# Token projections moved out of a memory chain, and transposes of a bulk stage spread and merged

## The chip, the cores and the metric

The kernel runs on one core of a Trainium2 chip, as one program, and computes a forward pass and all gradients. A core has TensorE (matmuls and transposes; in the profile PE, with its weight loads as PEld), VectorE (DVE), ScalarE (ACT), GpSimd (POOL) and SyncE (SP). SP only issues DMAs here; POOL computes and issues DMAs too. Transfers issued by SP appear under SPq. The metric is the device time of the program in microseconds (us), lower is better. The times stand for single executions; the profile shows one more execution.

## The reference, cut to what matters

A gate mixes two attentions over the same input, S = 2048 tokens of D = 576. Attention A is multi-query attention: 32 heads of 18, one shared key and value. Attention B is recurrent: 64 segments of 32 tokens, each preceded by 8 memory tokens that the segment before has produced; 32 heads of 128. The output is the forward result and the gradients of all inputs and weights (twelve arrays).

```python
def _A_ref(x, wq, wk, wv, wo):               # S = 2048, D = 576, H = 32, Dh = 18
    q = (x @ wq) in 32 heads;  k = x @ wk;  v = x @ wv
    p = _softmax(einsum('bhqd,bkd->bhqk', q, k) * Dh ** (-0.5))
    return heads_joined(einsum('bhqk,bkd->bhqd', p, v)) @ wo
def _B_ref(x, mem0, Wq, Wk, Wv, Wo, seg_len):  # M = 8, seg = 32, H = 32, Dh = 128
    mem = mem0
    for s in range(n_seg):                     # 64
        h = jnp.concatenate([mem, xs], axis=1)
        q, k, v = (einsum('btd,dhe->bhte', h, W) for W in (Wq, Wk, Wv))
        p = _softmax(where(mask, einsum('bhqe,bhke->bhqk', q, k) * scale, -1e9))
        o = einsum('bhte,hed->btd', einsum('bhqk,bhke->bhqe', p, v), Wo)
        mem = o[:, :M, :].copy();  outs.append(o[:, M:, :])
g = _sigmoid((x * gate_w).sum(-1, keepdims=True))
out = g * _A_ref(...) + (1 - g) * _B_ref(...)   # and its vjp with grad_out
```

(The listing is condensed; reshapes are left out.)

## The kernel before

`build_full` runs stages one after the other, each with its own SBUF and PSUM pools. In most of them a scheduler orders the instructions on each engine; the two woven stages and the bulk stage have their order written out by hand (`manual_schedule`), so their instructions go to each engine in the order of the Python code.

1. Preparation (`prep`), the setup of attention A (`a_weights`, `a_setup`, and `a_qd_all`, which projects queries and their gradients for 16 head pairs and 4 blocks of 512 tokens and stores them by SP), then `make_WoT`.
2. `b_proj_x(("dO",), ...)`: the output gradient of B times the transpose of Wo, for 16 tiles of 128 tokens. Each tile loads x transposed (`p_x`), runs 8 column groups of 512 with 5 k-tiles each (576 = 4 x 128 + 64; the last k-tile is filled up with zeros to 128 rows, both in the weights and in the tokens), evacuates `p_pb` in turns by DVE and ACT into `p_tok`, and stores it by SP. In each tile three pieces of W are transposed by DMA (`stash_WT`, 48 in all: SP transposes into `p_wt`, POOL stores `st_WT`) for use in the backward chain.
3. `load_W`, then `b_proj_x(("k", "v", "q"), ..., XT0)` with XT0 = 5: the same projection for the first 5 tiles, three weights each.
4. The forward chain of B, woven one to one with the first attention pass of A (`weave`: one piece of `b_chain_fwd`, one of `a_pass1`, 1024 pieces of the latter). The chain projects a segment's 8 memory tokens with Wk, Wq and Wv (`proj_part`): the 4096 columns are split into four quarters which sit in the four 32-column groups of the array, so the stationary operand `hm` has 32 columns, 8 of memory and 24 free. The free 24 columns carry ("ride") 24 of the tokens from tile 5 on, in every segment: 64 segments x 24 columns cover the remaining 11 tiles. `load_ride` brings them in; `rows_out` dumps the whole result to `row_dram` by POOL, and `rows_copy` copies from there, by SP, memory rows to `mtok` and token rows to `xtok`.
5. `a_out` (output projection of A: one token tile is loaded as `o_ot`, transposed on PE by `tok_T`, evacuated, multiplied in `row_mm` in columns 0 to 512 and 512 to 576) and `b_mem_fwd`.
6. `b_bulk`: the token rows of B, forward and backward, in 128 ticks of one token tile and a group of 4 heads. Nine stages work on successive groups, and each tick runs them in a fixed order: `st_QT` (transposes of q, k and dO on PE into PSUM tiles `x_tr`, which have two buffers), `st_S` (scores, exponentials on ACT, row sums and reciprocals on DVE), `st_T` (transposes of P), `st_O`, `st_OT` (transposes of o), `st_D`, `st_B`, `st_DT` (transposes of dS), `st_Q`, `st_K`. `transp`, used by `st_T` and `st_DT`, transposes four token blocks of 128 x 128 and four blocks of 128 x 32 memory scores, the latter one by one into the four row groups of a fifth block.
7. The backward chain of B woven with the second pass of A (it also uses `proj_part`), then `b_post`, `b_dw` and `a_final`, which again transposes token tiles with `tok_T` and multiplies them in `row_mm`.

`mm` (line 66 of the profile) and `tr` (line 71) are helpers that issue all matmuls and transposes, and `evac` (lines 61 and 63) copies PSUM to SBUF by DVE or ACT. The names in the profile tell which stage an instruction belongs to: p_ the dense projections, c_ the forward chain, a_ the attention A, x_ the bulk stage, o_ and z_ the stage after the chain, r_ the backward chain, f_ the final stage.

Of the kernel before, what the change touches and what calls it, by code (L numbers as in the profile page):

```python
# [11 lines left out]
P = 128  # L12

D = 576
# [16 lines left out]
class Kern:  # L31
# [50 lines left out]
    XT0 = 5  # L82

    def setup_B_dram(self, dram):
# [13 lines left out]
        self.row_dram = {w: t(w + "row_dram", [NSEG, P, 1024]) for w in ("k", "q", "v")}  # L98
# [13 lines left out]
    def zero_fill(self, sp):  # L112
        nc = self.nc
        z = sp.tile([P, 16, P], BF16, name="zfill")
        nc.gpsimd.memset(z[:], 0.0)
        for tt in range(self.NTT):
            nc.gpsimd.dma_start(self.pq_dram[tt].rearrange("s q c w k -> (s q c) w k"), z[:])

# [40 lines left out]
    def load_W(self, pool):  # L159
        nc = self.nc  # L160
        self.W = {}
        for w, src in (("k", self.B_Wk), ("q", self.B_Wq), ("v", self.B_Wv)):
            t = pool.tile([P, NKT, J], BF16, name="W" + w)
            nc.vector.memset(t[64:128, 4, :], 0.0)
            for kt in range(NKT):
                rows = KT_ROWS[kt]
                self.dq_eng().dma_start(t[0:rows, kt, :], src[kt * P:kt * P + rows, :])
            self.W[w] = t
# [13 lines left out]
    def b_proj_x(self, ws, srcT, sp, psum, ntt):  # L182
        nc = self.nc
        for tt in range(ntt):
            if len(ws) == 1:
                for c in range(3 * tt, 3 * tt + 3):
                    self.stash_WT(c, sp)
            xt = sp.tile([P, NKT, P], BF16, name="p_x", bufs=3)
            nc.sync.dma_start(xt[:], srcT[:, :, tt * P:(tt + 1) * P].rearrange("k p t -> p k t"))
            for w in ws:  # L190
                Wt = self.WoT if w == "dO" else self.W[w]
                tok = sp.tile([P, J], BF16, name="p_tok", bufs=2)
                for jc in range(8):
                    pb = psum.tile([P, 512], F32, name="p_pb", bufs=8)
                    for kt in range(NKT):
                        self.mm(pb[:], lhsT=xt[:, kt, :], rhs=Wt[:, kt, jc * 512:(jc + 1) * 512],
# [19 lines left out]
    def proj_part(self, pj, st, Wt, j, kts):  # L216
        for kt in kts:
            for c in range(4):
                self.mm(pj[32 * c:32 * c + 32, :], lhsT=st[:, kt, :],
                        rhs=Wt[:, kt, c * 1024 + j * 512:c * 1024 + (j + 1) * 512],  # L220
# [13 lines left out]
    def b_chain_fwd(self, keep, sp, psum):  # L234
# [8 lines left out]

        def ride(s):
            t0 = self.XT0 * P + 24 * s
            return t0, max(0, min(24, self.T - t0))

        def load_ride(s):
            t0, n = ride(s)
            if n:  # L250
                nc.sync.dma_start(hm[s % 2][:, :, 8:8 + n], self.xT_dram[:, :, t0:t0 + n].rearrange("k p t -> p k t"))

        load_ride(0)
# [14 lines left out]
        for s in range(NSEG):  # L268
# [8 lines left out]
            def rows_out(w):  # L277
                nc.gpsimd.dma_start(self.row_dram[w][s], t2[w][:].rearrange("p u e -> p (u e)"))

            def rows_copy(w):  # L280
                src = self.row_dram[w][s].rearrange("(c r) e -> c r e", r=32)
                t0, n = ride(s)
                nc.sync.dma_start(self.mtok[w][s * 8:(s + 1) * 8, :].rearrange("r (c e) -> c r e", c=4), src[:, 0:8, :])
                if n:
                    nc.sync.dma_start(self.xtok[w][t0:t0 + n, :].rearrange("r (c e) -> c r e", c=4), src[:, 8:8 + n, :])
# [9 lines left out]
            for j in range(2):  # L295
                proj("k", j)
                if j == 0 and s + 1 < NSEG:
                    load_ride(s + 1)
# [13 lines left out]
            rows_copy("k")  # L312
# [29 lines left out]
            rows_copy("q")  # L342
# [12 lines left out]
            if s + 1 < NSEG:  # L355
# [13 lines left out]
                rows_copy("v")  # L369
# [17 lines left out]
            else:  # L387
                yield
                rows_copy("v")
# [49 lines left out]
    def make_WoT(self, pool, psum):  # L439
        self.WoT = pool.tile([P, NKT, J], BF16, name="WoT")  # L440
        self.nc.vector.memset(self.WoT[64:128, 4, :], 0.0)
# [10 lines left out]
    def load_WoT(self, pool):  # L452
        self.WoT = pool.tile([P, NKT, J], BF16, name="WoT")
        self.nc.vector.memset(self.WoT[64:128, 4, :], 0.0)
# [9 lines left out]
    def b_bulk(self, wp, sp, psum):  # L464
# [76 lines left out]
        def transp(x, m, nm):  # L541
# [3 lines left out]
            for i in range(4):  # L545
                self.tr(pt[32 * i:32 * i + 32, 4, :], m[:, i, :], P, tp=(0, 32 * i))
# [14 lines left out]
        def st_QT(t):  # L561
            tt, g, r, d = view(t)
            for w, nb in (("q", 3), ("k", 3), ("dO", 6)):
                pt = psum.tile([P, 5, P], BF16, name="x_tr", bufs=2)
                for i in range(4):
                    self.tr(pt[:, i, :], d[w][:, 4 * (g % 4) + i, :], P)
                o = sp.tile([P, 4, P], BF16, name=f"x_{w}T", bufs=nb)
                self.evac(o[:], pt[:, 0:4, :], use="s" if w == "dO" else "v")
                sc[w + "T", t] = o
# [112 lines left out]
        order = list(enumerate(stages)) + [(6, st_K)]  # L682
        with self.tc.manual_schedule():
# [8 lines left out]
            for t in range(NG + len(stages) - 1):  # L692
                for n, st in order:
                    if 0 <= t - n < NG:
                        st(t - n)
                    if (n != 6 or st is st_K) and n in after and t - n >= 0 and (t - n) % 4 == 3:
# [40 lines left out]
    def b_chain_bwd(self, keep, sp, psum):  # L737
# [11 lines left out]
        def load(s):  # L749
# [15 lines left out]
            for w in ("k", "q"):  # L765
                nc.sync.dma_start(mrow[w][:].rearrange("p u e -> p (u e)"), self.row_dram[w][s])
# [345 lines left out]
    def setup_A_dram(self, dram):  # L1112
# [5 lines left out]
        self.dqtok_dram = dram.tile([T, D], BF16, name="dqtok_dram")  # L1118
        self.otok_dram = dram.tile([T, D], BF16, name="otok_dram")
# [20 lines left out]
    def prep(self, keep, xk, sp, psum):  # L1140
# [11 lines left out]
        nc.gpsimd.memset(self.daT[64:128, 4, :], 0.0)  # L1152
# [79 lines left out]
    def a_setup(self, keep, sp, psum):  # L1232
# [3 lines left out]
        for lo in range(0, T, 512):  # L1236
            pk = psum.tile([P, 512], F32, name="a_p1", bufs=2)
            for kt in range(NKT):
                self.mm(pk[:, :], lhsT=self.wkv[:, kt, :], rhs=self.xT[:, kt, lo:lo + 512],
# [50 lines left out]
    def a_qd(self, p, qb, sp, psum):  # L1290
# [3 lines left out]
        for kt in range(NKT):  # L1294
            self.mm(pq[0:64, :], lhsT=self.wqp[:, kt, p, :], rhs=self.xT[:, kt, q0:q0 + 512],
                    start=(kt == 0), stop=False, tp=(0, 0))
            self.mm(pq[64:128, :], lhsT=self.woTp[:, kt, p, :], rhs=self.daT[:, kt, q0:q0 + 512],
# [208 lines left out]

    def a_out(self, keep, sp, psum):
        nc = self.nc
        T, NTT = self.T, self.NTT
        wo = keep.tile([P, NKT, D], BF16, name="o_wo")  # L1510
        for kt in range(NKT):
            rows = KT_ROWS[kt]
            nc.sync.dma_start(wo[0:rows, kt, :], self.A_wo[kt * P:kt * P + rows, :])
        for tt in range(NTT):
            trows = slice(tt * P, (tt + 1) * P)
            ot = sp.tile([P, D], BF16, name="o_ot", bufs=3)
            nc.sync.dma_start(ot[:], self.otok_dram[trows, :])
            oT = self.tok_T(ot, sp, psum, "o")
            pa = psum.tile([P, 640], F32, name="o_pa", bufs=2)
            self.row_mm(pa, [(oT[0:KT_ROWS[kt], kt, :], wo[0:KT_ROWS[kt], kt, :]) for kt in range(NKT)])  # L1520
            a16 = sp.tile([P, D], BF16, name="o_a16", bufs=2)
            self.evac(a16[:, :], pa[:, 0:D])
            nc.gpsimd.dma_start(self.a_dram[trows, :], a16[:, :])

    def tok_T(self, tok, sp, psum, nm):
        ptr = psum.tile([P, NKT, P], BF16, name=nm + "_ptr", bufs=2)
        for kt in range(NKT):
            ncols = KT_ROWS[kt]
            self.tr(ptr[0:ncols, kt, :], tok[:, kt * P:kt * P + ncols], P)
        oT = sp.tile([P, NKT, P], BF16, name=nm + "_T", bufs=2)  # L1530
        self.evac(oT[:, 0:4, :], ptr[:, 0:4, :])
        self.evac(oT[0:64, 4, :], ptr[0:64, 4, :])
        return oT

    def row_mm(self, out, pairs):
        n = len(pairs)
        for (lo, hi) in ((0, 512), (512, D)):
            for i, (l, r) in enumerate(pairs):
                self.mm(out[:, lo:hi], lhsT=l, rhs=r[:, lo:hi], start=(i == 0), stop=(i == n - 1))

    def a_final(self, keep, sp, psum):
# [5 lines left out]
        for i, (nm, src) in enumerate((("x", self.A_x), ("dq", self.dqtok_dram), ("ot", self.otok_dram),  # L1547
                                       ("da", self.da_dram), ("dxb", self.dxB_dram))):
            t = keep.tile([P, NTT, D], BF16, name="f_" + nm)
            (nc.sync if i % 2 == 0 else nc.gpsimd).dma_start(t[:], src.rearrange("(n p) d -> p n d", p=P))  # L1550
# [11 lines left out]
        nc.sync.dma_start(dkv[:], self.dkv_dram[:, :])  # L1562
        wqT = keep.tile([P, NKT, D], BF16, name="f_wqT")
        wkvT = keep.tile([P, D], BF16, name="f_wkvT")
# [19 lines left out]
        for tt in range(NTT):  # L1584
            trows = slice(tt * P, (tt + 1) * P)
            dqT = self.tok_T(tok["dq"][:, tt, :], sp, psum, "f")
            pdx = psum.tile([P, 640], F32, name="f_big", bufs=2)
# [159 lines left out]
```

## Time and profile before

| what | us |
|---|---|
| median of 3 executions | 6764.76 |
| range of the 3 | 6764.18 to 6774.46 |
| the profiled execution | 6764.76 |
| its span | 6763.0 |

The mean granted TensorE clock is 0.965. By stage, from the windows of the trace:

| stage | from | to | us |
|---|---|---|---|
| preparation | 0 | 73 | 73 |
| attention A: weights, setup, queries | 73 | 234 | 161 |
| make_WoT | 234 | 256 | 22 |
| dO projection, with the stashed transposes | 256 | 441 | 185 |
| no matmul (the rest of the stash, then W) | 441 | 476 | 35 |
| k, v, q projection of 5 tiles | 476 | 637 | 161 |
| forward chain with pass 1 | 637 | 2625 | 1988 |
| a_out and b_mem_fwd | 2625 | 2740 | 115 |
| bulk | 2740 | 3525 | 785 |
| change to the next stage | 3525 | 3555 | 30 |
| backward chain with pass 2 | 3555 | 5374 | 1819 |
| b_post | 5374 | 5950 | 576 |
| b_dw | 5969 | 6633 | 664 |
| a_final | 6633 | 6763 | 130 |

The two woven stages are 56% of the span. In the list of groups below, each line gives the source line, engine, operation, output and inputs, count, busy time and mean duration, then the idle time in front and what ended most of it:

```profile
L1358 DVE TENSOR_TENSOR a_W<-a_dP,a_E 128x512 bf16<-128x512 f32 x2048 | 1312.5, 682 | 319.5 <-PE a_dP L66 257.7
L1328 ACT ACTIVATE a_E<-a_S 128x1024 bf16<-128x1024 f32 x1024 | 1050.7, 1026 | 248.8 <-PE a_dP L66 145.6
L66 PE MATMUL r_pj<-WT,r_dT 128*32 128x288 bf16 x12288 | 445.5, 287 | 0.0
L66 PEld LDWEIGHTS <-hm 128*32 128x32 bf16 x7680 | 210.5, 97 | 227.0 <-issue 16.3
```

The weight loads of `hm` are the chain's projections: 64 segments x 3 weights x 2 halves x 5 k-tiles x 4 quarters = 7680. A matmul's own duration in the trace is longer than its share of the time when matmuls follow each other, because they overlap; distances between starts give the pace. Where a helper issues everything, the tile names tell the stages apart.

### The profile page before, as it was taken

To read this page: it belongs to the slowest core of one execution; us is meant where nothing else is said; L and a number is where in the kernel's file an instruction comes from. 1 tells how busy PE (TensorE), PEld (TensorE's weight loads), DVE (VectorE), ACT (ScalarE), POOL (GpSimd) and SP (SyncE) were. 2 spreads that over 40 slices of the span, in tenths; PEclk is the share of its full clock that TensorE was granted. 3 is DMA by queue.
4 is the path that set the end of the run, shared out by engine and by line. 5 is a ranking of instruction groups with operands and counts; after the bars stand their busy time and mean duration, and the time that the engine had idled before them with its cause. 6 is when DMAs were issued, how large, how long until landed. Compare 5 with 4: busy or idle time off the path is not lost. (4 is left out here: it accounts for less than half of the span.)

```text
span 6763.0 us, 210460 instructions
## 1 busy us (share of the span) xinstructions
PE 6103.0 (90%) x89582; PEld 3364.9 (50%) x89798; DVE 3998.9 (59%) x7720; ACT 3372.0 (50%) x4881; POOL 1733.8 (26%) x3177
## 2 busy tenths in 40 slices
PE   6848999999999996699978999999999899989997
PEld 3313444444444443577763444444444488865443
DVE  4312788888788884455547888888888611111111
ACT  2212666666666664355545666666666522211100
POOL 3110222222222222344432222222222211112222
PEclk9979999999999998899999999999999899999998
DMA  5674444444444433788875434343343499976653
GB/s 179 197 241 126 89 90 94 89 93 88 93 88 93 90 83 96 211 245 245 249 225 168 99 99 98 99 99 100 99 99 99 114 252 252 252 266 215 221 177 107
DMA packets 1074116, 1000.44 MB, mean 148 GB/s; under 512 B 638269, under 2 KB 885894, under 8 KB 1061462
## 3 DMA queue, kind: packets, MB, share of 16 engines
q1 hardware_dynamic: 985078, 759.42, 44.3%
q0 software_dynamic: 88096, 227.54, 9.8%
q8 instruction: 703, 11.52, 0.7%
q14 instruction: 239, 1.96, 0.1%
HBM read 565.51 MB, written 386.86 MB: 141 GB/s over the span
## 5 line engine op out<-in xcount | busy, mean ns | idle before, releaser
L1358 DVE TENSOR_TENSOR a_W<-a_dP,a_E 128x512 bf16<-128x512 f32 x2048 | 1312.5, 682 | 319.5 <-PE a_dP L66 257.7
L1489 DVE TENSOR_TENSOR b_dS<-b_dP,b_E 128x512 bf16<-128x512 f32 x2048 | 1315.4, 684 | 311.5 <-PE b_dP L66 244.5
L1468 ACT ACTIVATE b_E<-b_S 128x1024 bf16<-128x1024 f32 x1024 | 1047.8, 1023 | 576.3 <-PE b_dP L66 409.4
L1328 ACT ACTIVATE a_E<-a_S 128x1024 bf16<-128x1024 f32 x1024 | 1050.7, 1026 | 248.8 <-PE a_dP L66 145.6
L66 PE MATMUL b_dP<-b_KV,b_QD 32*128 32x512 bf16 x2048 | 598.5, 384 | 20.1 <-DVE b_dS L1489 20.0
L66 PE MATMUL a_dP<-a_QD,l_KV 32*128 32x512 bf16 x2048 | 504.5, 382 | 15.2 <-DVE a_W L1358 15.0
L66 PE MATMUL b_S<-b_KV,b_QD 32*128 32x512 bf16 x2048 | 403.5, 387 | 105.0 <-ACT b_E L1468 58.2
L66 PE MATMUL w_acc<-w_d,w_h 128*128 128x512 bf16 (+1 forms) x2352 | 470.3, 380 | 2.5
L66 PE MATMUL r_pj<-WT,r_dT 128*32 128x288 bf16 x12288 | 445.5, 287 | 0.0
L66 PE MATMUL a_S<-a_QD,l_KV 32*128 32x512 bf16 x2048 | 399.9, 384 | 47.2 <-ACT a_E L1328 41.6
L66 PE MATMUL a_acc<-a_W,l_WK 128*32 128x512 bf16 x4096 | 411.0, 391 | 0.5 <-issue 0.4
L66 PE MATMUL b_acc<-b_dS,b_SD 128*32 128x512 bf16 x2048 | 408.6, 395 | 0.0
L66 PE MATMUL b_acc<-b_E,b_SD 128*32 128x512 bf16 x2048 | 408.2, 395 | 0.0
L66 PE MATMUL a_acc<-a_E,l_VK 128*32 128x512 bf16 x4096 | 400.0, 380 | 0.0
L66 PEld LDWEIGHTS <-r_dT 128*32 128x32 bf16 x12288 | 330.1, 97 | 78.4 <-issue 0.8
L971 DVE COPY y_T<-y_pt 128x512 bf16<-128x512 bf16 x256 | 96.9, 420 | 458.9 <-PE y_pt L71 458.9
L66 PEld LDWEIGHTS <-w_h 128*128 128x128 bf16 (+1 forms) x2400 | 212.1, 100 | 247.1 <-issue 6.3
L66 PEld LDWEIGHTS <-b_SD 128*32 128x32 bf16 x4096 | 105.4, 93 | 452.0 <-issue 451.9
L66 PEld LDWEIGHTS <-hm 128*32 128x32 bf16 x7680 | 210.5, 97 | 227.0 <-issue 16.3
L66 PEld LDWEIGHTS <-b_QD 32*128 32x128 bf16 x4096 | 142.7, 91 | 311.9 <-issue 227.1
L66 PEld LDWEIGHTS <-l_WK 128*32 128x32 bf16 x4096 | 105.5, 93 | 353.6 <-issue 353.5
L66 PE MATMUL y_pdx<-WT,y_T 128*128 128x288 bf16 x2048 | 271.8, 287 | 0.0
(426 smaller groups left out, 11446.0 us busy)
## 6 DMA issues: line engine op xcount, KB each, us to landing
b_QD<-qd_dram SPq DMA_DIRECT2D x256, 128.0 KB
b_SD<-sd_dram SPq DMA_DIRECT2D x256, 128.0 KB
dOx_dram<-p_tok SPq DMA_DIRECT2D x16, 1024.0 KB
c_vx<-vx_dram SPq DMA_DIRECT2D x256, 64.0 KB
krow_dram<-c_k POOLq DMA_DIRECT2D x64, 256.0 KB, 2.3
qrow_dram<-c_q POOLq DMA_DIRECT2D x64, 256.0 KB, 5.3
vrow_dram<-c_v POOLq DMA_DIRECT2D x64, 256.0 KB, 3.1
x_q<-qx_dram SPq DMA_DIRECT2D x32, 512.0 KB
```

Source lines behind the costliest of these rows:

```text
L66: return self.nc.tensor.matmul(out, lhsT, rhs, start=start, stop=stop, tile_position=tp, skip_group_check=True)
L971: nc.vector.tensor_copy(T_[t][w][:], pt[:])
L1328: nc.scalar.activation(E_[n][:], S.pop(n)[:], ACT.Exp, scale=SCALEA)
L1358: nc.vector.tensor_tensor(out=W_[n][:, i, :], in0=dP[i][:], in1=E_[n][:, i, :], op=ALU.mult)
L1468: nc.scalar.activation(E_[n][:], S.pop(n)[:], ACT.Exp, scale=SCALEA)
L1489: nc.vector.tensor_tensor(out=D_[n][:, i, :], in0=dP[i][:], in1=E_[n][:, i, :], op=ALU.mult)
```

## The change

- **Token projections.** `XT0` and the riding columns go. `b_proj_x` projects all 16 token tiles for k, v and q; in the chain the 24 free columns of `hm` carry nothing that is read. `load_ride`, `rows_copy` and `row_dram` vanish; `rows_out` sends the four quarters of the memory rows to `mtok` by POOL, and for k and q the whole result too (`mrow_dram`, for the backward chain).
- **The last k-tile.** It is used with its 64 rows instead of 128 with zeros, in `b_proj_x`, `proj_part`, `a_setup` and `a_qd`; the memsets that made the zeros go.
- **The stash.** `stash_WT` is called once per tile and weight of the k, v, q projection instead of three times per tile of dO. There the scheduler decides when each piece is issued.
- **Bulk.** `st_QT` transposes q alone; `st_KT` (k) comes after `st_O` and `st_GT` (dO) after `st_D`, both for the same group; xqT and xkT have two buffers instead of three. `transp` transposes the memory scores of four heads as one 128 x 128 block.
- **a_out and a_final.** The PE transposes are replaced by four DMA transposes of 512 x 640 each (new `tok_T`), for which `otok_dram` and `dqtok_dram` get 640 columns, the last 64 filled with zeros in `zero_fill`. `row_mm` works in two halves of 288 columns that share a stationary operand, instead of 512 and 64.

```diff
-    def b_proj_x(self, ws, srcT, sp, psum, ntt):
+    def b_proj_x(self, ws, srcT, sp, psum):
         nc = self.nc
-        for tt in range(ntt):
-            if len(ws) == 1:
-                for c in range(3 * tt, 3 * tt + 3):
-                    self.stash_WT(c, sp)
+        for tt in range(self.NTT):
             xt = sp.tile([P, NKT, P], BF16, name="p_x", bufs=3)
...
-            for w in ws:
+            for wi, w in enumerate(ws):
+                if len(ws) == 3:
+                    self.stash_WT(3 * tt + wi, sp)
...
-                        self.mm(pb[:], lhsT=xt[:, kt, :], rhs=Wt[:, kt, jc * 512:(jc + 1) * 512],
+                        rows = KT_ROWS[kt]
+                        self.mm(pb[:], lhsT=xt[0:rows, kt, :], rhs=Wt[0:rows, kt, jc * 512:(jc + 1) * 512],
...
     def proj_part(self, pj, st, Wt, j, kts):
         for kt in kts:
+            rows = KT_ROWS[kt]
             for c in range(4):
-                self.mm(pj[32 * c:32 * c + 32, :], lhsT=st[:, kt, :],
-                        rhs=Wt[:, kt, c * 1024 + j * 512:c * 1024 + (j + 1) * 512],
+                self.mm(pj[32 * c:32 * c + 32, :], lhsT=st[0:rows, kt, :],
+                        rhs=Wt[0:rows, kt, c * 1024 + j * 512:c * 1024 + (j + 1) * 512],
...
             def rows_out(w):
-                nc.gpsimd.dma_start(self.row_dram[w][s], t2[w][:].rearrange("p u e -> p (u e)"))
-
-            def rows_copy(w):
-                src = self.row_dram[w][s].rearrange("(c r) e -> c r e", r=32)
-                t0, n = ride(s)
-                nc.sync.dma_start(self.mtok[w][s * 8:(s + 1) * 8, :].rearrange("r (c e) -> c r e", c=4), src[:, 0:8, :])
-                if n:
-                    nc.sync.dma_start(self.xtok[w][t0:t0 + n, :].rearrange("r (c e) -> c r e", c=4), src[:, 8:8 + n, :])
+                for c in range(4):
+                    nc.gpsimd.dma_start(self.mtok[w][s * 8:(s + 1) * 8, c * 1024:(c + 1) * 1024], self.m_rows(t2[w], c))
+                if w != "v":
+                    nc.gpsimd.dma_start(self.mrow_dram[w][s], t2[w][:].rearrange("p u e -> p (u e)"))
...
             for i in range(4):
                 self.tr(pt[:, i, :], x[:, i, :], P)
-            for i in range(4):
-                self.tr(pt[32 * i:32 * i + 32, 4, :], m[:, i, :], P, tp=(0, 32 * i))
+            self.tr(pt[:, 4, :], m.rearrange("p i t -> p (i t)"), P)
...
-        def st_QT(t):
+        def trans(t, w, nb):
             tt, g, r, d = view(t)
-            for w, nb in (("q", 3), ("k", 3), ("dO", 6)):
-                pt = psum.tile([P, 5, P], BF16, name="x_tr", bufs=2)
-                for i in range(4):
-                    self.tr(pt[:, i, :], d[w][:, 4 * (g % 4) + i, :], P)
-                o = sp.tile([P, 4, P], BF16, name=f"x_{w}T", bufs=nb)
-                self.evac(o[:], pt[:, 0:4, :], use="s" if w == "dO" else "v")
-                sc[w + "T", t] = o
+            pt = psum.tile([P, 5, P], BF16, name="x_tr", bufs=2)
+            for i in range(4):
+                self.tr(pt[:, i, :], d[w][:, 4 * (g % 4) + i, :], P)
+            o = sp.tile([P, 4, P], BF16, name=f"x_{w}T", bufs=nb)
+            self.evac(o[:], pt[:, 0:4, :], use="s" if w == "dO" else "v")
+            sc[w + "T", t] = o
+
+        st_QT = lambda t: trans(t, "q", 2)
+        st_KT = lambda t: trans(t, "k", 2)
+        st_GT = lambda t: trans(t, "dO", 6)
...
         order = list(enumerate(stages)) + [(6, st_K)]
+        order.insert(4, (0, st_KT))
+        order.insert(7, (0, st_GT))
...
+    def tok_T(self, srcd, pool, nm):
+        t = pool.tile([P, NKT, self.T], BF16, name=nm)
+        for q in range(4):
+            r = slice(q * self.T // 4, (q + 1) * self.T // 4)
+            self.nc.sync.dma_start_transpose(t[:, :, r], srcd[r, :])
+        return t
...
     def row_mm(self, out, pairs):
         n = len(pairs)
-        for (lo, hi) in ((0, 512), (512, D)):
-            for i, (l, r) in enumerate(pairs):
-                self.mm(out[:, lo:hi], lhsT=l, rhs=r[:, lo:hi], start=(i == 0), stop=(i == n - 1))
+        for i, (l, r) in enumerate(pairs):
+            for hf in range(2):
+                self.mm(out[:, hf, 0:288], lhsT=l, rhs=r[:, 288 * hf:288 * hf + 288], start=(i == 0), stop=(i == n - 1))
...
```

In `a_qd` and `a_setup` the operands are cut to `[0:rows]` in the same way; `a_out` and `a_final` take slices `oT[:, kt, trows]` and `dqT[:, kt, trows]` of the transposed whole.

## The prediction

> **What bounds the kernel now.** I read the busy totals first, then a table of windows by stage, then the timeline inside the stages that the diff touches. Totals:
>
> ```profile
> span 6763.0 us, 210460 instructions
> PE 6103.0 (90%) x89582; PEld 3364.9 (50%) x89798; DVE 3998.9 (59%) x7720; ACT 3372.0 (50%) x4881; POOL 1733.8 (26%) x3177
> ```
>
> TensorE is busy for 90%, so a matmul added in a dense stage lengthens the span nearly one for one, and one removed helps only where PE sets the pace. By stage (window, us, then busy PE, PEld, DVE, ACT, POOL, clock, DMA share, GB/s):
>
> ```profile
> 256.00:441.00 185.00, 146.07 (x627) 64.29 (x640) 39.97 (x62) 33.83 (x63) 21.09 (x39) 0.91 0.80 226
> 441.00:476.00 35.00, 0.00 (x0) 0.00 (x0) 5.11 (x6) 1.03 (x3) 7.49 (x14) 0.54 0.66 209
> 637.00:2625.00 1988.00, 1901.38 (x34010) 889.37 (x34011) 1583.23 (x2944) 1347.08 (x1790) 555.08 (x1216) 0.99 0.43 90
> 2740.00:3525.00 785.00, 697.84 (x10627) 552.02 (x10752) 444.35 (x1041) 415.09 (x912) 335.23 (x425) 0.97 0.83 236
> ```
>
> They are the dO projection, a wait for W, the forward chain woven with the first attention pass, and the bulk stage. The first two are held by DMA; the chain leaves PE idle for 87 us of 1988; bulk for 87 of 785. The timeline then gives each price (start, us, engine, line, operation, count, idle before and its releaser):
>
> ```profile
> 558.58 8.80 PE L66 MATMUL p_pb<-Wk,p_x 128*128 128x512 bf16 x39
> 567.21 8.80 PE L66 MATMUL p_pb<-Wv,p_x 128*128 128x512 bf16 x39
> ...
> 464.89 0.54 POOL L180 DMA_DIRECT2D st_WT<-p_wt  x1 [4.66 <-DMA p_wt<-in_B_Wv_dram]
> 468.64 0.54 POOL L180 DMA_DIRECT2D st_WT<-p_wt  x1 [3.21 <-DMA p_wt<-in_B_Wv_dram]
> 471.04 1.37 SPq L167 DMA_DIRECT2D Wk<-in_B_Wk_dram  x3
> 476.24 0.58 PE L66 MATMUL p_pb<-Wk,p_x 128*128 128x512 bf16 x1 [35.38 <-DMA Wk<-in_B_Wk_dram]
> ...
> 1520.83 1.25 PE L66 MATMUL c_pj<-Wk,hm 128*32 128x512 bf16 x20
> 1522.01 0.39 PE L66 MATMUL a_S<-a_QD,l_KV 32*128 32x512 bf16 x2
> ```
>
> One token tile of one weight takes 567.21 − 558.58 = 8.63 us: 40 matmuls of 0.2158. The stashed transposes of W end at 468.64 and only then is W loaded. In the chain, 20 projection matmuls go four abreast, 5 × 0.2158 = 1.08, but the next matmul stands 1.18 after the first: 0.10 for changing the array's tiling.
>
> **What the Trainium skill says.** "TensorEngine Tiling (Array Packing)", section Tiling Modes, Key Properties: changing the tiling mode drains TensorE. The 0.10 above agrees. "TensorE: Matmul & The Clock Gate", section on packing small matmuls: matmuls start and end strictly in program order; so a matmul that waits for a buffer holds everything behind it. The bulk timeline below, where no matmul passes a waiting one, agrees. "DMA: Bandwidth & Descriptors", section DMA Transpose (X-bar): a plain DMA transpose goes only on SP's or ACT's queue; the trace has them on SPq (11.49 us for three at 435.60), so new ones queue with SP's loads and stores.
>
> **The change, part by part.** Sums are against the profiled execution, 6764.76 us (span 6763.0 and 1.8 around it), which equals the median of the three runs.
>
> (a) Riding tokens. Before, k, v, q are projected for 5 tiles densely; the other 11 ride in spare stationary columns of the chain's projections, at no PE time. After, all 16 are dense: 11 × 3 × 8.63 = **+285**. Nothing overlaps: PE was busy 133.23 of the 161 us from 476 to 637, and within the loop matmuls follow without a gap. The chain's matmuls stay as many and as long (moving size 512, whatever columns carry).
>
> (b) The last k-tile has 64 rows instead of 128 with zeros. Each 512-column group of 5 matmuls then changes tiling there and back. The nearest row is the final stage, where 4 matmuls of 128 rows, one of 64, then one of 128 (f_dkv) come in turn:
>
> ```profile
> 6705.41 1.36 PE L66 MATMUL f_big<-f_wqT,f_T 128*128 128x512 bf16 x5
> 6706.37 0.09 PEld L66 LDWEIGHTS <-f_T 64*128 64x128 bf16 x1 [0.42 <-DVE f_T L61]
> 6706.70 0.39 PE L66 MATMUL f_big<-f_wkvT,f_dkv 128*128 128x512 bf16 x1
> ```
>
> The five take 6706.70 − 6705.41 = 1.29 us instead of 1.08: 0.20 per excursion. k, v, q: 48 × 8 = 384 excursions, **+77**. Bounds 0 (a dense stream may hide it) and 0.25.
>
> (c) dO projection. The 48 transposes left this loop (1.3 us on SP and one POOL store each, about one per 4.5 us: 48 from 256 to 469). PE's own work is 16 × 8.63 = 138, plus 128 excursions = 26: it ends near 420 with W issued near 424, not 471: **−47** (−30 to −50).
>
> (d) Where those transposes go. The diff puts them into the k, v, q loop, but in the built order SP has ten of them in the preparation, three with the first attention's weights, about 21 alternating one to one with the query stores of its setup, and 14 at the head of dO. In the setup a query store falls due every 3.75 us, a stash takes 4.5: 22 × 0.75 = 16; POOL's stores of the stash stand in front of a memset and of stores that later work needs. **+15** (0 to +40). Slicing rows in that setup: +5 (0 to 13).
>
> (e) Forward chain. Ride loads and row copies leave SP; POOL gets 11 more DMAs per segment, at 0.54 us each 6 of a segment's 31 us, where POOL is 28% busy: hidden. Without that cover (if POOL's normalisation of the first attention's rows came late by it) it would cost up to 6 × 64 = 384. 384 projections (64 segments × 3 weights × 2 halves) each get one more tiling change (the change back was paid already, to the 32-row scores): 384 × 0.10 = 38, less 2: **+36** (0 to +75).
>
> (f) a_out. PE transposes and evacuations go; four crossbar transposes on SP come, one ahead of the 128 loads that precede the stage, and row products go in halves of 288. Its 115 us have PE busy 53, held by DMA round trips, and memory tokens keep a cycle of about 8.4 us: **−15** (−30 to +10).
>
> (g) Bulk. A tick is 3111.57 − 3105.79 = 5.78 us, 128 times. The lines that matter:
>
> ```profile
> 3106.70 0.38 PE L71 MATMUL x_tr<-identB,x_dO 128*128 128x128 bf16 x4 [0.29 <-DVE x_qT L61]
> 3108.45 0.39 PE L71 MATMUL x_tr<-identB,x_o 128*128 128x128 bf16 x4
> 3108.46 0.82 DVE L586 TENSOR_REDUCE x_l<-x_E 128x4 f32<-128x640 bf16 x1 [1.48 <-ACT x_E L584]
> 3109.39 0.18 DVE L588 RECIPROCAL x_r<-x_l 128x4 f32<-128x4 f32 x1
> 3109.48 0.46 DVE L548 COPY x_PT<-x_tr 128x640 bf16<-128x640 bf16 x1
> 3110.31 0.39 PE L71 MATMUL x_tr<-identB,x_dS 128*128 128x128 bf16 x4
> ```
>
> Removed: the wait before dO (0.45 with the gap), and eight quarter-width transposes of memory scores become two full ones, about 0.2 for each four (0.26 before, 0.06 after), 0.4 a tick. Added: the k transposes now stand between T and OT, and x_tr has two buffers, so OT reuses the buffer that T filled and must wait until x_PT is copied. DVE's order has x_PT behind x_l and x_r, which wait for this tick's exponentials. Scores start at 3106.92, x_PT ends at 3109.94: 3.02 later. So OT starts at +3.08 (before: +1.53). From OT to the next q took 3.12; less 0.2, plus 0.22 for dO, 3.14; q itself 0.22. Tick 3.08 + 3.14 + 0.22 = 6.44, so 128 × 0.65 = **+83**. Queued behind the waiting OT is all of the tick's rest, and DVE has only x_kT (0.41) to do meanwhile. If the wait does not bite: −0.85 × 128 = −109.
>
> (h) Backward chain: row slices on 64 segments × 2 projections, one more switch of 0.10 each, **+13** (0 to 26). (i) a_final: transposes leave PE, crossbar ones go behind f_dkv's load at 6668: **−10** (−25 to +10).
>
> Sum: 285 + 77 − 47 + 15 + 5 + 36 − 15 + 83 + 13 − 10 = +442; 6765 + 442 = **7207 us**.
>
> **Rivals.** R1: the bulk wait doesn't bite, because DVE gets to x_PT early or the exponentials come sooner. For it: one stall of 0.45 a tick and 0.4 of PE work do vanish. Against: the order on DVE and the buffer. 442 − 83 − 109 = +250: 7015 us.
>
> R2: a 64-row matmul in a dense stream costs no drain. For it: in the row above the 64-row load also waited for its copy. Against: the next token tile, which starts at 6707.31, shows no such wait and takes 1.28, the same 0.2. 442 − 77 − 26 − 36 − 13 − 5 = +285: 7050. With R1 about 6860.
>
> R3, faster: the forward chain is really paced by the ride copies. A weave piece takes 1988/1024 = 1.94 us; where the pass runs alone, near the stage's end, scores start every 1.55 us in the timeline (2613.41, 2614.96). If the copies held the difference, the stage falls by 0.39 × 1024 = −400; the kernel gets faster once the piece is below 1.51 us (442/1024 less). Against: PE is 96% busy in that stage.
>
> R4: the riding was worth nothing, part (a) being hidden by the loads: excluded, since PE was busy 83% there.
>
> **How the numbers follow.** Main case 55%, R1 20%, R2 15%, both 5%, R3 3%, the rest slower still. The range goes from R1's value, 7010, to the upper ends of (d) and (e), 7280. A difference under about 0.2% can't be told from none: chances faster 0.03, within 0.2% 0.01, slower 0.96.
>
> **What would show it.** k, v, q tiles every 10.2 us per weight (8.63 in R2); that stage some 490 us long; dO ending near 420 with W at once behind; transposes on SPq in the first 250 us; chain pieces of 1.98 us; bulk ticks of 6.44 with x_o transposes idle 1.3 us on DVE x_PT (R1: 4.95 and no such wait). I am wrong if the chain stage shrinks by hundreds of us, if POOL's new DMAs become the chain's releaser, or if the stashes stall the setup by more than 40.

## The result and the profile after

The kernel after takes 7160.16 us (median of 4 executions, 7156.98 to 7168.28) against 6767.60 for the kernel before on the same chip: ratio 1.0581, 95% interval 1.0562 to 1.0599. The forecast was 7207 with a range of 7010 to 7280. The profiled execution has a span of 7154.9 us, 391.9 more than before.

The totals and the windows of the kernel after, which answer to those of before (columns as there):

```profile
span 7154.9 us, 211949 instructions
PE 6493.4 (91%) x89962; PEld 3444.5 (48%) x90190; DVE 4086.5 (57%) x7817; ACT 3460.7 (48%) x4981; POOL 2091.7 (29%) x3882
272.00:437.00 165.00, 163.93 (x627) 51.20 (x637) 44.28 (x64) 37.26 (x64) 5.94 (x11) 1.00 0.47 155
437.00:446.00 9.00, 0.00 (x0) 0.00 (x0) 0.00 (x0) 0.24 (x1) 3.70 (x7) 0.62 0.69 256
446.00:970.00 524.00, 498.54 (x1881) 156.25 (x1920) 132.44 (x192) 112.17 (x192) 0.00 (x0) 0.97 0.32 123
970.00:2985.00 2015.00, 1934.46 (x34010) 880.60 (x34011) 1583.04 (x2944) 1347.57 (x1790) 910.71 (x1915) 0.99 0.27 65
3100.00:3942.00 842.00, 659.79 (x9858) 543.46 (x9984) 455.75 (x1040) 438.54 (x912) 336.82 (x402) 0.98 0.78 221
```

These are dO, the wait for W, the k, v, q projection, the forward chain and the bulk stage. dO no longer waits for DMA (PE busy 163.93 of 165), the wait for W has shrunk from 35 to 9 us, k, v, q has grown from 161 to 524, and in bulk PE's busy time has fallen by 38 while the stage has become 57 longer: a new wait.

For an account without overlaps I take marks in both traces: the first matmul of dO and of k, the first and last exponential of each woven stage, the first q transpose of bulk.

| between | before | after | difference | forecast |
|---|---|---|---|---|
| start, first dO matmul | 256.2 | 271.7 | +15.5 | (d) +20 |
| first dO matmul, first k matmul | 220.0 | 174.7 | -45.3 | (c) -47 |
| first k matmul, first exponential of pass 1 | 185.5 | 544.4 | +358.9 | (a) and (b) +362 |
| pass 1, first to last exponential | 1955.3 | 1987.2 | +31.9 | (e) +36 |
| to the first q transpose of bulk | 123.3 | 122.9 | -0.4 | (f) -15 |
| bulk, to the first exponential of pass 2 | 810.9 | 869.1 | +58.2 | (g) +83 |
| pass 2, first to last exponential | 1818.7 | 1796.3 | -22.4 | (h) +13 |
| to the end | 1393.1 | 1388.6 | -4.5 | (i) -10 |

The sum is +391.9. Here are the two mechanisms that the forecast rested on, in the timeline of the kernel after. First the k, v, q projection (start, us, engine, line, operation, count, idle before it and its releaser):

```profile
691.22 10.38 PE L66 MATMUL p_pb<-Wk,p_x 128*128 128x512 bf16 x39
696.05 0.09 PEld L66 LDWEIGHTS <-p_x 64*128 64x128 bf16 x1 [0.42 <-issue]
696.37 0.55 PEld L66 LDWEIGHTS <-p_x 128*128 128x128 bf16 x4 [0.23 <-issue]
697.34 0.09 PEld L66 LDWEIGHTS <-p_x 64*128 64x128 bf16 x1 [0.42 <-issue]
697.66 0.55 PEld L66 LDWEIGHTS <-p_x 128*128 128x128 bf16 x4 [0.23 <-issue]
701.52 10.37 PE L66 MATMUL p_pb<-Wv,p_x 128*128 128x512 bf16 x39
```

A tile of one weight takes 10.3 us instead of 8.63. The weight loads (PEld) show where the time goes: in every group of five the loading stands idle for 0.42 us ahead of the one with 64 rows and for 0.23 ahead of the next one, and groups follow each other by 1.29 us (696.37 to 697.66) instead of 1.08. In the kernel before the loads come without such gaps:

```profile
557.93 3.12 PEld L66 LDWEIGHTS <-p_x 128*128 128x128 bf16 x15
```

Then a tick of bulk in the kernel after:

```profile
3505.01 0.38 PE L71 MATMUL x_tr<-identB,x_P 128*128 128x128 bf16 x4
3505.23 0.22 PE L71 MATMUL x_tr<-identB,x_Pm 128*128 128x128 bf16 x1
3505.73 0.39 PE L71 MATMUL x_tr<-identB,x_k 128*128 128x128 bf16 x4
3505.80 0.82 DVE L565 TENSOR_REDUCE x_l<-x_E 128x4 f32<-128x640 bf16 x1 [0.86 <-ACT x_E L563]
3506.81 0.46 DVE L524 COPY x_PT<-x_tr 128x640 bf16<-128x640 bf16 x1
3507.32 0.38 PE L71 MATMUL x_tr<-identB,x_o 128*128 128x128 bf16 x4 [1.21 <-DVE x_PT L524]
```

The x_o transposes wait 1.21 us for x_PT, which DVE copies only after the row sums x_l. The scores begin at 3504.31, so x_o starts 3.01 us after them. One tick lasts 6.37 us (the median over the stage), where it was 5.79.

### The profile page after: what moved, and what is told of

Read it like the earlier page. It is cut to its first block, busy times and chain, and to the rows that moved or that the text cites. A ratio compares the mean times of both kernels' runs of the same rounds, so it can differ in the third digit from the quotient of the medians.

```text
span 7154.9 us, 211949 instructions
## 1 busy us (share of the span) xinstructions
PE 6493.4 (91%) x89962; PEld 3444.5 (48%) x90190; DVE 4086.5 (57%) x7817; ACT 3460.7 (48%) x4981; POOL 2091.7 (29%) x3882
## 5 line engine op out<-in xcount | busy, mean ns | idle before, releaser
L66 PE MATMUL b_dP<-b_KV,b_QD 32*128 32x512 bf16 x2048 | 600.0, 382 | 12.6 <-DVE b_dS L1471 12.5
L66 PE MATMUL b_S<-b_KV,b_QD 32*128 32x512 bf16 x2048 | 401.0, 384 | 86.0 <-ACT b_E L1450 39.6
L61 DVE CAST p_tok<-p_pb 128x512 bf16<-128x512 f32 x256 | 176.7, 692 | 520.8 <-PE p_pb L66 520.8
L66 PEld LDWEIGHTS <-p_x 128*128 128x128 bf16 (+1 forms) x2560 | 207.7, 97 | 490.7 <-issue 366.1
L63 ACT CAST p_tok<-p_pb 128x512 bf16<-128x512 f32 x256 | 149.9, 586 | 548.9 <-PE p_pb L66 548.9
L66 PEld LDWEIGHTS <-hm 128*32 128x32 bf16 (+1 forms) x7680 | 205.4, 95 | 345.7 <-issue 149.7
```

Source lines behind the costliest of these rows:

```text
L61: nc.vector.tensor_copy(out, in_)
L63: nc.scalar.copy(out, in_)
L66: return self.nc.tensor.matmul(out, lhsT, rhs, start=start, stop=stop, tile_position=tp, skip_group_check=True)
```

## The experiments

All times are medians of four or more executions, ratios against the kernel before on the same chip. Measured along with the different runs, the kernel before took 6763.1 to 6768.2 us, so a few us between a run and the kernel after mean nothing. Where pieces of a stage are quoted, they lie between the same marks as above, in one profiled execution of each kernel.

**1. Merged memory scores alone.** The kernel before with one edit:

```diff
-            for i in range(4):
-                self.tr(pt[32 * i:32 * i + 32, 4, :], m[:, i, :], P, tp=(0, 32 * i))
+            self.tr(pt[:, 4, :], m.rearrange("p i t -> p (i t)"), P)
```

> The kernel before, with one edit: the memory scores of four heads are transposed at once. Theory (PE sets the tick): two groups of four become one transpose each, 0.2 us less for each, tick 5.79 to 5.39 us, 51 us in all, about 6715 us. Rival (something else ends the tick, DVE, ACT or the DMAs at 83% busy): tick stays at 5.79 and the time at 6767.

6720.45 us, ratio 0.9931 (0.9916 to 0.9946). The median tick is 5.35, as the theory has it; some ticks are longer, so bulk gains 41 us, not 51. This part of the change is a gain by itself.

**2. The new order alone.** The kernel before with `st_QT` split and

```diff
         order = list(enumerate(stages)) + [(6, st_K)]
+        order.insert(4, (0, st_KT))
+        order.insert(7, (0, st_GT))
```

> The kernel before, with one edit: the order of the bulk transposes of the kernel after (q first, k between O and OT, dO after D), without the merged memory scores. Theory (the buffer that T wrote makes OT wait for x_PT on DVE): tick 6.37 + 0.2 for the longer DT = 6.57 us (T's 0.2 is inside the wait), +100 us, about 6868 us. Rival (the longer tick comes from the merged transposes): the wait before dO is gone and the tick falls to 5.34, about 6710 us.

6865.14 us, ratio 1.0141 (1.0122 to 1.0159), and a tick of 6.59. In its timeline x_o waits for the same copy:

```profile
3111.34 0.46 DVE L548 COPY x_PT<-x_tr 128x640 bf16<-128x640 bf16 x1
3111.85 0.38 PE L71 MATMUL x_tr<-identB,x_o 128*128 128x128 bf16 x4 [0.99 <-DVE x_PT L548]
```

So the order does the harm, the merge does not, and the wait before dO, which the order removes, was the cheaper of the two.

**3. Another order.** The kernel after with

```diff
-        order.insert(4, (0, st_KT))
-        order.insert(7, (0, st_GT))
+        order.insert(1, (0, st_KT))
+        order.insert(8, (0, st_GT))
```

Now q, T and k, OT share the two buffers in turn, k is copied ahead of the row sums, and dO takes T's buffer only after the long `st_B`.

> The kernel after, with the bulk order q, k, S, T, O, OT, D, B, dO, DT, Q, K, in which no transpose takes the buffer of T or waits for DVE's row sums. Theory: the tick becomes PE's own work, about 4.9 us instead of 6.37, 188 us less, about 6972 us. Rival (DMA is next: 78% busy at 6.37, which is 5.0 us of work a tick; or ACT): tick 5.1 to 5.4, about 7000 to 7035 us. If the wait on x_PT isn't the cause, the tick stays near 6.4.

7051.01 us, ratio 1.0418 (1.0401 to 1.0436) to the kernel before, 109 us less than the kernel after. The wait on x_PT is gone and the median tick is 4.92, as the theory says, but the stage gains 111 us and not 188: 33 of the ticks last 6 to 9 us, and in them stores are waited for. Four lines picked from the list of waits of this run between 3160 and 3800 us (engine, line, what for: us in total, times, longest):

```profile
POOL x_P L570 <- DMA px_dram<-x_P: 55.2, 14, 6.2
DVE x_dS L628 <- DMA dsx_dram<-x_dS: 42.6, 21, 4.3
PE x_m L66 <- DVE x_dSm L628: 35.8, 19, 4.0
ACT x_o L533 <- DMA ox_dram<-x_o: 30.3, 22, 3.5
```

And its window within bulk, below that of the same stage in run 1:

```profile
2790.00:3450.00 660.00, 617.19 (x9466) 508.22 (x9464) 411.36 (x985) 393.60 (x865) 303.90 (x364) 1.00 0.90 253
```

```profile
3160.00:3800.00 640.00, 590.58 (x9129) 496.17 (x9126) 406.09 (x951) 389.40 (x835) 294.34 (x353) 0.98 0.92 253
```

Both move 253 GB/s. From the first to the last q transpose run 1 takes 714 us and run 3 takes 702, although the median tick differs by 0.43 us: with PE's waits out of the way, the transfers seem to bound the stage. The rival of this run named that cause and was 16 us too hopeful about the size. It is argued from the equal rate and the waits; no run changed the transfers alone.

**4. Rows filled up again.** The kernel after with 128 rows in every last k-tile, and the memsets that zero them, for instance

```diff
-                        rows = KT_ROWS[kt]
-                        self.mm(pb[:], lhsT=xt[0:rows, kt, :], rhs=Wt[0:rows, kt, jc * 512:(jc + 1) * 512],
+                        self.mm(pb[:], lhsT=xt[:, kt, :], rhs=Wt[:, kt, jc * 512:(jc + 1) * 512],
```

> The kernel after, with the last k-tile filled up to 128 rows again everywhere. Theory (a 64-row matmul drains the array twice, 0.1 each): the k, v, q stage falls from 524 to 447 us, dO from 165 to 139, the forward chain's pieces from 1987 to 1955, the backward chain doesn't change: about 7025 us. Rival (64 rows cost nothing, the stages are longer for other reasons): no change, 7160. Open: the backward chain ran 22 us faster than before; if the slices do that it returns to 1819 us, if not it stays at 1796.

7019.56 us, 141 less than the kernel after. k, v, q take 444.9 us from the first k to the last q instead of 522.8 (-77.9), dO to k 148.1 instead of 174.7 (-26.6), pass 1 1952.5 instead of 1987.2 (-34.7), the setup 2.9 less. Its k, v, q tiles are at the old pace again:

```profile
602.98 8.80 PE L66 MATMUL p_pb<-Wk,p_x 128*128 128x512 bf16 x40
611.61 8.80 PE L66 MATMUL p_pb<-Wv,p_x 128*128 128x512 bf16 x40
620.24 8.80 PE L66 MATMUL p_pb<-Wq,p_x 128*128 128x512 bf16 x40
```

Half of a k-tile saved nothing and cost 0.2 us each time. The backward pass stayed at 1794.4: it isn't the rows that made it faster.

**5. The transposes of W back in dO.** The kernel after with

```diff
+            if len(ws) == 1:
+                for c in range(3 * tt, 3 * tt + 3):
+                    self.stash_WT(c, sp)
...
-                if len(ws) == 3:
-                    self.stash_WT(3 * tt + wi, sp)
```

> The kernel after, with the 48 stashed transposes back in the dO projection, three per tile. Theory: query setup 15 us shorter (dO starts near 256 instead of 272), then dO and the wait for W 45 us longer (k starts 220 us after dO, as before, instead of 175): +30, about 7190 us. Rival (dO was longer for another reason than the stash): k starts 175 us after dO, 7145 us.

7200.79 us, 41 more than the kernel after. dO to k becomes 216.8 again (+42.1), as expected. But dO starts at 267.5, only 4.2 earlier: beside the cut rows, the transposes among the query stores cost 4 us and not 15.

**6. Riding tokens back.** The kernel after with `XT0`, `load_ride` and `rows_copy` as before, and 5 tiles in the k, v, q projection (the 48 transposes spread over its 15 weights). The core of it:

```diff
-                    k.b_proj_x(("k", "v", "q"), k.xT_dram, pxs, pxp)
+                    k.b_proj_x(("k", "v", "q"), k.xT_dram, pxs, pxp, k.XT0)
```

> The kernel after, with 24 tokens per segment riding in the forward chain again and only 5 token tiles projected densely; rows stay cut to 64. Theory: 11/16 of the k, v, q stage goes, 285 + 53 for its share of tiling changes = 338 us, and the chain's pieces stay at 1987 us, since the ride copies were hidden before and POOL's additional DMAs are hidden after: about 6822 us. Rival (the copies paced the chain): its pieces grow to more than 1995. Open: backward pieces, 1819 before and 1796 after; they return to 1819 if it is the rides' data or copies that slow them.

6838.53 us, ratio 1.0100 (1.0083 to 1.0117), 322 less than the kernel after. From the first k to the first exponential it takes 205.6 us instead of 544.4 (-338.8). The time is 17 over the expectation. In the profiled execution, which took 10 us more than the median of this run, the setup is 12 longer and pass 1 takes 2002.5, 15 more and past the mark that was set for the rival. This doesn't show that the rides' transfers pace the chain: in pass 1 of this trace the granted clock stands at half for 32.7 us in seven stretches, in that of the kernel after for 7.5 us in two. Where PE sets the pace, half of the difference is lost, an estimated 12.6 of the 15 us. With padded rows no cost of the rides shows: pass 1 takes 1949.5 to 1959.0 us in the seven profiles with rides and 1952.5 without (run 4). The backward pass stays at 1793.8.

**7. Memory tokens ahead of a_out.** The kernel after with

```diff
-            k.a_out(aok, aos, aop)
             k.b_mem_fwd(aos, aop)
+            k.a_out(aok, aos, aop)
```

> The kernel after, with the memory tokens (z_) called ahead of a_out. Theory: a_out stands still for 50 us after the first pass, on the small stores and the crossbar loads, and the memory tokens, which need none of it, now come after it; put ahead they lie inside that wait, and the bulk begins 30 to 40 us earlier: about 7125 us. Rival (their loads queue on SP behind the same stores): no change, 7160 us.

7137.88 us, 22 less. The instructions of both by tile (count: durations, first and last start), for the kernel after and then for this one:

```profile
L66 PE MATMUL o_pa<-o_wo,o_T x160: 282/286/444, 3027.7 to 3056.9; 128*128 128x288 bf16 x160
L414 POOL DMA_DIRECT2D om_dram<-z_tk x4: 532/632/727, 3060.7 to 3091.6; - x4
```

```profile
L66 PE MATMUL o_pa<-o_wo,o_T x160: 286/286/448, 3029.7 to 3072.5; 128*128 128x288 bf16 x160
L414 POOL DMA_DIRECT2D om_dram<-z_tk x4: 540/744/750, 3044.1 to 3072.8; - x4
```

In the kernel after the products of a_out end 32 us sooner than before (78.9 us after the last exponential, 110.6 before), and then the memory tokens begin, which before ran between them. Side by side they save 18 us of the stage; they don't start within the 50 us of waiting (PE's first work for the memory tokens comes at 3028.3 us, a_out's at 3029.7), so the expected 30 to 40 is missed.

**8. Spare columns filled.** The kernel after with

```diff
-            nc.vector.memset(hm[i][:], 0.0)
+            nc.vector.memset(hm[i][:], 0.05)
```

> The kernel after, with the 24 spare columns of the chain's memory tile filled with 0.05 instead of 0; no result depends on them, they only reach rows that are multiplied by zeros. Theory (before, riding tokens put values other than zero into operands of the backward chain, and the granted clock dips more): backward pieces return from 1796 to about 1819 us, and the time is about 7182 us. Rival (the dips come from elsewhere: phase or copies): 1796, 7160 us.

7156.95 us, backward pass 1795.7. The data of the spare columns play no part.

**9. Crossbar parts alone.** The kernel before with the new `tok_T`, `row_mm`, a_out, a_final and `zero_fill`, and the arrays of 640 columns.

> The kernel before, with only the crossbar transposes of a_out and a_final, their half rows and the zero filling of the widened arrays. Theory: a_out's own gain (30 us of its stage) is given back by the memory tokens behind it, the final stage gains 4, so 6763 or no change; the rest of the later start of the dO projection (11 us with the stash back and rows cut, of which 3 are the cuts) comes from the zero filling, so dO starts near 264 instead of 256, and the sum is about 6770. Open: backward pieces; 1819 (crossbar has no part in them) or 1796 (the moved arrays or the final transposes do).

6732.69 us, ratio 0.9947 (0.9930 to 0.9964). dO starts at 258.0, so the zero filling costs about 2 us, not 8. The way from the last exponential to bulk takes 123.6, unchanged, as expected. The gain comes from stages that this edit doesn't touch: the backward pass takes 1791.3 us (-27) and bulk 801.1 (-10). The next section says what the traces show of this.

**10. The parts that gain.** The kernel before with the edits of runs 1, 7 and 9, and the transposes of W called from the k, v, q projection; rides, padded rows and the bulk order stay as before.

> The parts of the change that gain, without those that lose: riding tokens and padded rows as before, bulk order as before with merged memory scores, transposes of W called from the k, v, q projection, crossbar transposes, and the memory tokens ahead of a_out. Sum of what the runs gave: -47 (merged scores), -45 + 4 to 15 (transposes of W), -18 (memory tokens first), -4 (final) = about -105, 6660 us. Rival (the parts get in each other's way, the bulk stage being at 90% DMA already): over 6690.

6610.17 us, ratio 0.9766 (0.9747 to 0.9785): faster than both kernels, by more than was expected. The stages: setup +11.3, dO to k -71.7 (with padded rows the whole of the transposes' cost shows, PE alone needs 138), a_out and memory tokens -15.2, bulk -52.9, backward pass -23.3, the rest within 4 each.

**11 and 12. Two tries at the backward pass.** The kernel before, first with only the two arrays widened, then with four of a_out's loads cut in two:

```diff
-        self.dqtok_dram = dram.tile([T, D], BF16, name="dqtok_dram")
-        self.otok_dram = dram.tile([T, D], BF16, name="otok_dram")
+        self.dqtok_dram = dram.tile([T, NKT * P], BF16, name="dqtok_dram")
+        self.otok_dram = dram.tile([T, NKT * P], BF16, name="otok_dram")
...
```

(Left out: the loads from them take columns 0 to D.)

> The kernel before, with only the two arrays otok and dqtok widened from 576 to 640 columns in HBM, the last 64 never touched; all instructions stay, only the addresses of the arrays behind them move. Theory (where arrays lie in HBM sets the backward chain's dips): backward pieces 1795 us and about 6743 us. Rival (the crossbar transposes themselves, or the pools of a_out and a_final, do it): 1819 us, 6767 us.

6764.87 us, ratio 1.0002 (0.9994 to 1.0011), backward pass 1817.8.

```diff
-            nc.sync.dma_start(wo[0:rows, kt, :], self.A_wo[kt * P:kt * P + rows, :])
+            for lo in range(0, rows, 64):
+                nc.sync.dma_start(wo[lo:lo + 64, kt, :], self.A_wo[kt * P + lo:kt * P + lo + 64, :])
```

> The kernel before, with four of the five weight loads of a_out cut into two, so that SP issues four DMAs more ahead of the bulk stage and every later SP DMA counts on another of the eight completion semaphores that are used in turn (by four places, as with the crossbar parts); nothing else changes. Theory (the place in this rotation sets which transfers wait for each other, and with it the late segments of the backward chain): backward pieces 1795 us and about 6743 us. Rival (the rotation has no part): 1819 us, 6766 us.

6768.05 us, ratio 0.9999 (0.9990 to 1.0008), backward pass 1817.4. Neither place in memory nor SP's place in the rotation of semaphores is the cause.

## Why the prediction was right, and where it was not

The direction, the order of size and the two main mechanisms held. No rival did: the wait on x_PT bites (R1), 64 rows cost 0.2 us each in a dense stream (R2; run 4), and the chain's pieces didn't get shorter (R3). The forecast of +442 is 50 above the measured +391.9. The large misses are (g) and (h), 25 and 35 too high, and (f), 15 too low, which offsets a part by luck. In (g) and (h) the crossbar parts, that is the DMA transposes of a_out and a_final with what belongs to them, changed stages that they don't touch, which the forecast had at nothing.

- **(a) and (b).** +362 forecast, +358.9 measured, and runs 4 and 6 give the parts: 77.9 for the rows (77 forecast), 338.8 for eleven tiles with their share of the rows (338).
- **(c).** -47 forecast, -45.3 measured; run 5 puts it on the transposes. PE's own 164 us, as summed, then bound the stage.
- **(d).** The sum of +20 came near the +15.5, partly by luck: the terms of 15 for the transposes and 5 for the rows are not what the runs show. Zero filling, which wasn't counted, costs 1.8 (run 9, dO at 258.0). On top of it the transposes alone cost 9.5 (run 10, 267.5) and the cut rows alone also 9.5 (run 5, 267.5), but both together 13.7 (the kernel after, 271.7). So each seems to hide a part of the other, and taking one away from the kernel after gives back only 4.2 (run 5) or 2.9 (run 4); profiles with the same setup differ by up to 2.6 us.
- **(e).** +36 forecast, +31.9 measured. The cut rows make +34.7 (run 4); the other -3 is less than pass 1 differs among profiles in which it is the same (1949.5 to 1959.0). POOL's new DMAs raise its busy time from 555 to 911 us and cost nothing that shows.
- **(f).** -15 forecast, -0.4 measured: a_out got 32 us shorter as a run of products, and the stage did not. The forecast saw that memory tokens keep a pace of their own, but counted on their staying interleaved; the order put them behind (run 7).
- **(g).** +83 forecast, +58.2 measured. The tick was sized well: 6.37 against 6.44, since x_o starts at 3.01 and not 3.08 after the scores. That is 0.58 x 128 = +74. The mis-sized term is the start of the stage, which wasn't counted: the first four intervals between q transposes took 31.1 us instead of 42.3, which is 11 of the 16 us between +74 and +58.2. The order didn't do that. They take 28.9 to 33.4 us in the nine profiles with the crossbar parts, run 9 among them, which leaves bulk as it was, and 42.1 to 43.8 in the five without, run 2 among them, which has the order. How the crossbar parts do it was not tried.
- **(h).** +13 forecast, -22.4 measured. The row term doesn't show in the time: run 4 without it has 1794.4 against 1796.3. It is spent inside PE's waits for exponentials: over the backward pass they are 50.2 us in run 4 and 39.6 in the kernel after (the two lines below the list, in this order: us, times, longest). The gain belongs to the crossbar parts (run 9), which touch neither this stage nor its operands.
- **(i).** -10 forecast, -4.5 measured.

```profile
PE b_S L66 <- ACT b_E L1450: 50.2, 203, 1.2
PE b_S L66 <- ACT b_E L1450: 39.6, 139, 1.2
```

How do the crossbar parts speed up the backward pass? In the trace of before every second segment begins late, by 0.35 us or by about 1.3. These late heads make 22 of the 27 us between before and run 9. At those of 1.3 us the granted clock falls to half for 3.4 us. After the first 50 us of the pass there are 12 to 15 such stretches in the five profiles without the crossbar parts and 0 to 4 in the nine with them. Here is one head of a segment in the timeline and its window, in the kernel before:

```profile
4164.39 1.51 PE L66 MATMUL r_pj<-WoT,dm 128*32 128x512 bf16 x12
```

```profile
4164.00:4167.50 3.50, 3.50 (x33) 0.87 (x32) 2.07 (x4) 1.65 (x2) 0.88 (x1) 0.55 0.15 40
```

And the same head in the kernel after:

```profile
4576.62 0.82 PE L66 MATMUL r_pj<-WoT,dm 128*32 128x512 bf16 x12
```

```profile
4576.40:4580.00 3.60, 3.56 (x47) 1.07 (x49) 3.02 (x5) 2.96 (x4) 0.87 (x1) 1.00 0.34 46
```

The same twelve matmuls take 1.51 us at a granted clock of 0.55 and 0.82 us at 1.00. All runs with the crossbar parts have 1791 to 1796 us between the marks, all runs without 1815 to 1821, whatever else they change. Cut rows, rides, spare data, addresses in HBM and SP's count of DMAs are ruled out by runs 4, 6, 8, 11 and 12.

The traces show where the head gets late. Just ahead of it DVE stands idle for 0.56 us in the kernel before, and a packet of instructions is loaded (the second line, from the DMA queues between 4162.5 and 4164.5 us):

```profile
4162.51 1.29 DVE L1489 TENSOR_TENSOR b_dS<-b_dP,b_E 128x512 bf16<-128x512 f32 x2 [0.56 <-PE b_dP L66]
q14 instruction: 1, 0.01, 1.1%
```

At the same place of run 9 no such packet is loaded within 1 us ahead of the head, and DVE stands idle for 0.21 us, though the PE work that both lines name ends at the same distance from the head (1.63 us):

```profile
4153.19 1.29 DVE L1491 TENSOR_TENSOR b_dS<-b_dP,b_E 128x512 bf16<-128x512 f32 x2 [0.21 <-PE b_dP L66]
```

In the backward pass of every profile one such packet, of 8 KiB, comes as a rule with each 128 of DVE's instructions (waits counted too), and two segments hold 128 of them, so it meets the same place of every second segment. In the five profiles without the crossbar parts DVE has 6024 instructions ahead of the pass, and the packet comes within 1 us ahead of the late heads, where DVE's idle time is 0.55 to 0.58 us; at the other heads it is 0.21. In the nine with the crossbar parts the number is another (5997 to 6139), the packet comes 4 to 9 us after a head, and the idle time is 0.21 at nearly all heads. The packet itself starts 0.67 us after DVE's wait has ended, so what ties the two is the place in DVE's instructions, not the transfer's own time. By these traces the gain in this pass comes from where the packets fall, an accident of how many instructions stand ahead, and not from the DMA transposes as such. It is read from fourteen traces; no run changed DVE's count of instructions alone. Why the clock falls at some of the late heads and not at others stays open.

## What to carry to other kernels

When work is spread in a hand-written order, follow each shared PSUM buffer round its rotation, and then follow the engine that frees it back through its own queue: here two buffers made PE wait for a copy that stood behind a row sum. A contraction cut from 128 rows to its true 64 saved nothing on TensorE here and cost 0.2 us each time in a dense stream; filling up with zeros was cheaper by 141 us (run 4). Work that rides in free stationary columns showed no cost, and taking it out shows at full price. A gain in a stage that the change doesn't touch is no merit of the change until the traces say where it comes from.

## What the runs showed of the hardware

- A matmul of 64 rows between matmuls of 128 costs 0.20 to 0.21 us more than a full one in a dense stream (8.63 to 10.3 us for eight of them among 40).
- In the backward pass the cut rows cost nothing that shows (1796.3 us, padded 1794.4 in run 4), and PE's waits for ScalarE are 10.6 us shorter with them (39.6 instead of 50.2).
- With PE's waits removed, the bulk stage stands at 253 GB/s and 90 to 92% busy DMA engines in two different orders.
- In the backward pass a packet of 8 KiB on the queue q14 (instruction) comes as a rule with every 128 of DVE's instructions (fourteen profiles). Where it fell just ahead of a segment's head, DVE stood idle for 0.56 us instead of 0.21.
- An edit in stages long past moved that place and changed the time of an untouched stage by 1.5% (1818.7 to 1791.3 us, run 9); every profile with the crossbar parts shows it.
